# The first layer of 128-row expert blocks as seven products of row halves, on one Trainium2 core

## The chip, the cores and the metric

The kernel runs on one core of a Trainium2 chip. A core has engines that run side by side, each through its own queue in order: TensorE (PE, with its weight loads as PEld), VectorE (DVE), ScalarE (ACT), GpSimd (POOL) and SyncE (SP), and DMA queues. They wait for each other by semaphores. The metric is the device time of one execution in microseconds; three runs of the kernel before gave 626.19, 626.38 and 627.47, median 626.38.

## What is computed

Causal attention over a window of 64 positions, for 8 batches of 576 positions and 8 heads of 64, gives x with 8 x 576 = 4608 rows of 512. Then each row goes to one of eight experts:

```
logits = x @ w_gate                       # 512 -> 8
local  = sigmoid(x @ w_local)
e      = argmax(logits) if s == 0 or local < 0.5 else e of the row before
p      = softmax(logits)
h      = maximum(x @ w1[e], 0)            # 512 -> 1024
out    = p[e] * (h @ w2[e])               # 1024 -> 512
```

All in float32. Which rows belong to which expert is known only while the kernel runs.

## The kernel before

The attention part writes x to DRAM and works out each row's expert. Then the rows of each expert are cut into blocks, and each block fetches its rows by indirect DMAs (gathers, issued by POOL) and the two weight matrices of its expert by DMAs from SP's queue (2 MB each). There are four kinds of block:

- large, 256 rows (two slots of 128), numbers below `NB`;
- of 128 rows (one slot), numbers from `NB` to below `KINDS[1]`; four of them stand in the order of this program;
- of 64 rows (halves), from `KINDS[1]` to below `KINDS[2]`;
- of 32 rows (quarters), from `KINDS[2]`.

The order is made by `run`: large blocks one after the other, and behind every second one a smaller block. A block of 128 rows always stands between two large ones. `rows` sets the kind of a block in a dictionary `st`: `rows` (rows of a slot), `big`, `fast1` and `fast2` (whether the first and the second layer go by seven products).

Each block goes through four steps. `turn` (VectorE) transposes the gathered rows into `st["xt"]`, 128 partitions x 4 x rows: x turned, so that the contraction lies on the partitions. `prepare` (VectorE, where `fast1` is set) makes the sums and differences that the seven products need. `hidden` is the first layer and writes `h`, 128 x 8 x rows. `result` is the second layer, scales it by p[e] and scatters the rows to the output.

Seven products: a matrix product cut into quarters needs eight products of quarters; by Winograd's form of Strassen's scheme seven will do, with sums of quarters of the one matrix (`ws`, from `left`), differences of quarters of the other (`xs`, from `right`), and additions of the products. `big_hidden` does this for x @ w1: it cuts w1 by its contraction (two halves of 256) and its columns (two halves of 512), and x by contraction and by rows. Three PSUM banks, `px`, `py`, `pz`, hold the products; ScalarE keeps copies of three of them in SBUF (`keep`), VectorE adds a copy to a later product, ScalarE applies the relu, and so the four quarters of h, `hq[i][j]` (i: half of the 1024 columns, j: half of the rows), are made one after the other, from the fourth, fifth, sixth and seventh product. `big_result` does the same for h @ w2; its `put` is a VectorE instruction that scales and adds a piece of the output, three in a block, and between its products it calls hooks, in which VectorE's work for the next block is issued. The fifth of these hooks, behind the second `put`, makes the sums `s3` and `s4` of the next block if `turn` left them for later (`rest`).

A block of 128 rows has neither: its first layer is the plain loop in `hidden`, 8 x 4 matmuls of 128x128 weights against 128 columns, in two PSUM tiles. The first is emptied by ScalarE while the second is filled, the second by VectorE (`tensor_relu`, L1525). Its second layer is the plain loop at the end of `result`, 8 matmuls with 512 columns, of which the first four read the first half of `h`'s columns and the last four the second half. A block of 64 rows runs the same loop in `hidden` with `st["rows"]` = 64: the weights of a 128-column tile are cut in two halves of 64 columns, which write partitions 0 to 63 and 64 to 127 of PSUM (side by side).

In this part of the kernel all engines run in the order in which the code is written (`manual_schedule`). The names `ws1`, `xs` and `keep0` to `keep2` are single buffers. A gather is released by the matmul at which `pace` is called: in `hidden` behind every second column tile, in `big_hidden` behind every product.

## Time and profile before

One execution was profiled: it took 627.78 us, of which the span from the first to the last instruction is 626.0 us.

| | |
|---|---|
| median of three runs | 626.38 us |
| the profiled execution | 627.78 us |
| its span | 626.0 us |
| TensorE's mean granted clock | 0.999 |
| bytes moved by DMA | 165.80 MB, mean 265 GB/s |

The attention part fills about the first quarter of the span, the experts the rest. In the profile's lists "x64" counts records; a float32 matmul leaves two of them, with a weight load each. A row of an order of time gives the start, the time from there to the end of the last record merged into the row, engine, line, operation, and in brackets the idle time before it and what ended it. Matmuls overlap at their ends, so lengths are best read from start to start. A row of the groups by line gives, behind the bar, the busy time in us, the mean of one record in ns, and the idle time before.

### The profile page before, as it was taken

The numbers are of one execution on the slowest core, as the hardware profiler recorded it, in microseconds if no ns is written. First come the engines' busy times: TensorE is split into PE (matmuls) and PEld (weight loads), VectorE is DVE, ScalarE is ACT, GpSimd is POOL, SyncE is SP. The second block draws the span as 40 slices with busy tenths as digits, with TensorE's granted clock in tenths as the row PEclk, the third lists the DMA queues.
The fourth block names the chain that finished last, engine by engine and source line by source line (L and its number), as shares of the span: only waits on it lengthen the run. The fifth ranks groups of instructions, "written<-read, shape, count | busy, mean of one in ns | idle before, by whom it ended". The sixth has DMA issues, their size and how long they took to land. (4 is left out here: it accounts for less than half of the span.)

```text
span 626.0 us, 15072 instructions
## 1 busy us (share of the span) xinstructions
PE 600.5 (96%) x6253; PEld 528.9 (84%) x6253; DVE 403.2 (64%) x757; ACT 200.5 (32%) x368; POOL 271.4 (43%) x261
## 2 busy tenths in 40 slices
PE   7888988999999999999999999999999999999995
PEld 6677766788889999979899799978997998999994
DVE  6567579888996767347381885183926763886730
ACT  3766755722382232203130123112221322123120
POOL 4432111622102567437146775175275866452001
PEclk9999999999999999999999999999999999999999
DMA  8999998787945557476967866687768656955601
GB/s 328 401 415 407 365 378 284 273 304 250 385 153 186 190 210 281 170 272 246 394 245 259 321 198 217 230 314 300 299 239 316 256 189 223 403 193 208 233 18 40
DMA packets 31880, 165.80 MB, mean 265 GB/s; under 512 B 10531, under 2 KB 12217, under 8 KB 22586
## 3 DMA queue, kind: packets, MB, share of 16 engines
q1 hardware_dynamic: 20394, 135.54, 58.6%
q0 software_dynamic: 11408, 29.20, 13.0%
q8 instruction: 51, 0.84, 0.5%
q14 instruction: 27, 0.22, 0.1%
HBM read 145.52 MB, written 19.59 MB: 264 GB/s over the span
## 5 line engine op out<-in xcount | busy, mean ns | idle before, releaser
L1184 POOL DMA_INDIRECT xg<-xs,g x118 | 134.2, 1138 | 46.0 <-issue 25.3
L1494 POOL DMA_INDIRECT out_dram<-y,idx x36 | 41.1, 1142 | 161.3 <-DVE y L1425 68.5
L1414 PE MATMUL hp<-ws,hs 128*128 128x256 f32 x384 | 88.9, 380 | 0.0
L1414 PEld LDWEIGHTS hp<-ws,hs 128*128 128x128 f32 x384 | 72.5, 190 | 10.9 <-issue 1.2
L1363 PE MATMUL hp<-xs,ws 128*128 128x128 f32 x672 | 79.7, 275 | 0.0
L1363 PEld LDWEIGHTS hp<-xs,ws 128*128 128x128 f32 x672 | 77.3, 192 | 0.1
L1425 DVE SCALAR_TENSOR_TENSOR y<-hp,pws,kept 128x256 f32<-128x256 f32 x48 | 23.2, 482 | 68.2 <-issue 41.2
L1514 PE MATMUL hp<-xt,w 128*64 128x64 f32 (+2 forms) x640 | 66.2, 276 | 0.0
L1514 PEld LDWEIGHTS hp<-xt,w 128*128 128x128 f32 (+1 forms) x640 | 60.8, 170 | 4.1 <-issue 0.7
L1414 PE MATMUL hp<-w,h 128*128 128x256 f32 x256 | 60.5, 379 | 0.0
L1375 DVE TENSOR_TENSOR h<-hp,keep 128x512 f32<-128x512 f32 x42 | 28.6, 689 | 43.9 <-PE hp L1363 43.1
L1363 PEld LDWEIGHTS hp<-xt,w 128*128 128x128 f32 x448 | 53.2, 192 | 2.7 <-issue 2.3
L1363 PE MATMUL hp<-xt,w 128*128 128x128 f32 x448 | 54.7, 275 | 0.0
L394 PEld LDWEIGHTS sp<-w 64*64 64x64 f32 x1296 | 39.1, 135 | 16.2 <-issue 11.2
L1414 PEld LDWEIGHTS hp<-w,h 128*128 128x128 f32 x256 | 47.3, 190 | 5.7
L425 ACT ACTIVATE p<-sp 128x512 f32<-128x512 f32 x72 | 39.1, 596 | 37.1 <-PE sp L394 34.8
L440 PE MATMUL xo<-vb,p 128*64 128x74 f32 (+1 forms) x576 | 44.0, 228 | 6.9 <-DVE x L450 3.0
L394 PE MATMUL sp<-w 64*64 64x128 f32 (+1 forms) x1296 | 45.1, 267 | 5.7 <-issue 4.5
L430 DVE TENSOR_TENSOR p<-p,mask 128x1024 f32<-128x1024 f32 x29 | 35.8, 1235 | 22.4 <-ACT p L425 22.3
L1184 POOL DMA_INDIRECT pws<-xw,gx x40 | 44.3, 1107 | 13.2 <-issue 8.5
L440 PEld LDWEIGHTS xo<-vb,p 128*64 128x64 f32 x576 | 38.3, 136 | 12.6 <-issue 5.2
L1376 ACT ACTIVATE h<-h 128x512 f32<-128x512 f32 x42 | 26.3, 630 | 60.1 <-DVE h L1375 60.1
(287 smaller groups left out, 977.5 us busy)
## 6 DMA issues: line engine op xcount, KB each, us to landing
w<-in_w_dram SPq DMA_DIRECT2D x22, 2048.0 KB, 9.4
w<-in_w1t_dram SPq DMA_DIRECT2D x20, 2048.0 KB, 8.7
w<-in_kq_dram SPq DMA_DIRECT2D x17, 1024.0 KB, 11.2
w<-in_w_dram SPq DMA_DIRECT2D x24, 512.0 KB, 8.5
xs<-x POOLq DMA_DIRECT2D x9, 1024.0 KB, 5.9
va<-in_v_dram SPq DMA_DIRECT2D x5, 1184.0 KB, 7.5
vtt<-in_vt_dram SPq DMA_DIRECT2D x5, 1024.0 KB, 6.2
va<-in_v_dram SPq DMA_DIRECT2D x3, 1040.0 KB, 15.5
```

The source lines that it names most:

```text
L394: nc.tensor.matmul(sp[j][c * WIN:(c + 1) * WIN, a:b], lhsT=kt[h, hp, block * WIN:(block + 1) * WIN], rhs=qt[h, hp, a:b], start=not biased, ...
L425: nc.scalar.activation(p[:, j], sp[j], Act.Exp, scale=DH ** -0.5)
L430: masked.append(nc.vector.tensor_tensor(p, p, m.to_broadcast([P, 2, SC]), op=Alu.mult))
L440: nc.tensor.matmul(xo[par * WIN:(par + 1) * WIN, j, s * VW:s * VW + n], lhsT=p[:, j, b * WIN:(b + 1) * WIN], rhs=w[:, s, 2 * hp + j, :n], ...
L1184: return self.nc.gpsimd.indirect_dma_start(out=out, out_offset=None, in_=table[:rows, :], in_offset=bass.IndirectOffsetOnAxis(ap=idx, axis=0))
L1363: mm = nc.tensor.matmul(out[:, m, :], lhsT=a[:, kk, m * P:(m + 1) * P], rhs=b[:, kk, :], start=start and m + kk == 0, stop=stop and (m, kk ...
L1375: nc.vector.tensor_tensor(o, x, y, op=add)
L1376: nc.scalar.activation(o, x if y is None else o, Act.Relu)
L1414: mm = nc.tensor.matmul(out, lhsT=a[:, m, :], rhs=b[:, m, :], start=start and m == 0, stop=stop and m == FK // 2 - 1, skip_group_check=True)
L1425: nc.vector.scalar_tensor_tensor(o, x, pw[i], y2, Alu.mult, Alu.add)
L1494: return self.nc.gpsimd.indirect_dma_start(out=self.out[:, :], out_offset=bass.IndirectOffsetOnAxis(ap=st["idx"][:, s:s + 1], axis=0), in_ ...
L1514: mm = nc.tensor.matmul(hp[a, i, :], lhsT=st["w1"][:, kk, m * P:(m + 1) * P][:, a], rhs=st["xt"][:, kk, :n], start=(kk == 0), stop=(kk == ...
```

## The change

Blocks of 128 rows (`fast1` now depends on `n < KINDS[1]`, so all blocks with 128 rows in a slot) do their first layer by `big_hidden`, with row halves of 64 instead of 128 (`st["wide"]`). Each product has 4 column tiles x 2 contraction steps, and each matmul is cut in two with 64 weight columns, which write the two halves of the partitions. The second layer stays plain, so `prepare2` and `halves`, which serve it, are left out for these blocks. `sums` keeps the size of its tile and hands out a narrower part.

```diff
@@ rows
-        st.update(x=[], slots=slots, idx=idx, rows=P, big=len(slots) == 2, fast1=len(slots) == 2 and n not in PLAIN1,
+        st.update(x=[], slots=slots, idx=idx, rows=P, big=len(slots) == 2, fast1=n < KINDS[1] and n not in PLAIN1,
                   fast2=len(slots) == 2 and n not in PLAIN2)
+        st["wide"] = P if st["big"] else HF
@@ prepare
-        st["xq"] = quarters(st["xt"], DK, BIG)
+        c = 2 * st["wide"]
+        st["xq"] = quarters(st["xt"][:, :, :c], DK, c)
         st["xt"] = self.right("xs", st["xq"])
@@ sums
-        t = self.one.tile([P, 4, a[0][0].shape[1], a[0][0].shape[2]], F32, name=name)
-        return [t[:, i] for i in range(4)]
+        n, c = a[0][0].shape[1:]
+        t = self.one.tile([P, 4, n, max(c, P)], F32, name=name)
+        return [t[:, i, :, :c] for i in range(4)]
@@ big_hidden
-        self.prepare2(st)
+        if st["fast2"]:
+            self.prepare2(st)
+        n, c = FK // 2, st["wide"]
         st["h"] = h = self.wk.tile([P, FK, BIG], F32, name="h", bufs=1)
-        st["hq"] = hq = quarters(h, FK, BIG)
-        n = FK // 2
-
-        pz, py, px = (self.ps_h.tile([P, n, P], F32, name="hp") for _ in range(3))
+        st["hq"] = hq = quarters(h[:, :, :2 * c], FK, 2 * c)
+
+        pz, py, px = (self.ps_h.tile([P, n, P], F32, name="hp")[:, :, :c] for _ in range(3))
 
         def product(out, a, b, start=True, stop=True):
             for m in range(n):
                 for kk in range(DK // 2):
-                    mm = nc.tensor.matmul(out[:, m, :], lhsT=a[:, kk, m * P:(m + 1) * P], rhs=b[:, kk, :],
-                                     start=start and m + kk == 0,
-                                     stop=stop and (m, kk) == (n - 1, DK // 2 - 1), skip_group_check=True)
+                    for f in range(0, P, c):
+                        mm = nc.tensor.matmul(out[f:f + c, m, :], lhsT=a[:, kk, m * P + f:m * P + f + c],
+                                              rhs=b[:, kk, :], start=start and m + kk == 0,
+                                              stop=stop and (m, kk) == (n - 1, DK // 2 - 1), skip_group_check=True)
             self.pace(mm)
 
         def keep(i, x):
-            o = self.one.tile([P, n, P], F32, name=f"keep{i}")
+            o = self.one.tile([P, n, P], F32, name=f"keep{i}")[:, :, :c]
...
         relu(hq[1][0], px)
         step()
-        self.halves(st)
+        if st["fast2"]:
+            self.halves(st)
```

The lines shift by up to six: L1363 of before is L1368 of the change, L1566 is L1572, L1425 is L1431, L1514 is L1520.

TensorE's queue in the first block of 128 rows before: the plain first layer (L1514, into `hp`) and the second layer (L1566, into `yp`), each row with the semaphores for which its first matmul waits.

```order
L1514 MATMUL hp<-xt,w 128x128 [waits DMAHW1_49]
L1514 MATMUL hp<-xt,w 128x128 x15
L1514 MATMUL hp<-xt,w 128x128 [waits DVE_49]
L1514 MATMUL hp<-xt,w 128x128 x15
L1566 MATMUL yp<-w,h 128x512 [waits DMAHW2_49,Activation_49]
L1566 MATMUL yp<-w,h 128x512 x3
L1566 MATMUL yp<-w,h 128x512 [waits DVE_49]
L1566 MATMUL yp<-w,h 128x512 x3
```

The same place of the change, from the third product on:

```order
L1368 MATMUL hp<-xs,ws_3507 64x64 [waits Activation_49]
L1368 MATMUL hp<-xs,ws_3507 64x64 x15
L1368 MATMUL hp<-xt,w 64x64 x16
L1368 MATMUL hp<-xs,ws_3507 64x64 [waits Activation_49]
L1368 MATMUL hp<-xs,ws_3507 64x64 x15
L1368 MATMUL hp<-xt,ws_3507 64x64 x16
L1368 MATMUL hp<-xs,w 64x64 [waits DVE_49]
L1368 MATMUL hp<-xs,w 64x64 x15
L1572 MATMUL yp<-w,h 128x512 [waits DMAHW2_49,Activation_49]
L1572 MATMUL yp<-w,h 128x512 x3
L1572 MATMUL yp<-w,h 128x512 [waits Activation_49]
L1572 MATMUL yp<-w,h 128x512 x3
```

Thirty-two matmuls of 128x128 become seven products of sixteen with 64x64; products wait for ScalarE's copies and VectorE's additions, and the second layer's first matmul waits for a later relu of ScalarE than before, since both row halves must be there.

VectorE's queue ahead of the same block and in it, before: the transpose of its rows, the three `put` of the large block ahead (L1425), the relu (L1525).

```order
L1283 STREAM_TRANSPOSE xt<-xg 128x4x4x32 [waits DMASW2_49,DMASW3_49,DMASW1_49,DMASW0_49]
L1425 SCALAR_TENSOR_TENSOR y<-hp,pws,kept_3512 128x256 [waits DMASW1_49,DMASW6_49,PE_49,Activation_49]
L1425 SCALAR_TENSOR_TENSOR y<-hp,pws,kept_3518 128x256 [waits DMASW4_49,DMASW7_49,PE_49,Activation_49]
L1425 SCALAR_TENSOR_TENSOR y<-hp,pws,kept_3524 128x256 [waits PE_49,Activation_49]
L1525 TENSOR_SCALAR h<-hp 128x4x128 [waits DVE_49,PE_49]
```

In the change, behind the same transpose:

```order
L1328 TENSOR_TENSOR xs<-xt 128x2x64
L1328 TENSOR_TENSOR xs<-xt,xs 128x2x64 [waits DVE_49]
L1314 TENSOR_TENSOR ws_3507<-w 128x1024 [waits DMAHW1_49]
L1314 TENSOR_TENSOR ws_3507<-ws_3507,w 128x1024 [waits DVE_49]
L1431 SCALAR_TENSOR_TENSOR y<-hp,pws,kept_3520 128x256 [waits DMASW1_49,DMASW6_49,PE_49,Activation_49]
L1431 SCALAR_TENSOR_TENSOR y<-hp,pws,kept_3526 128x256 [waits DMASW4_49,DMASW7_49,PE_49,Activation_49]
L1314 TENSOR_TENSOR ws_3507<-w 128x1024
L1314 TENSOR_TENSOR ws_3507<-w,ws_3507 128x1024 [waits DVE_49]
L1431 SCALAR_TENSOR_TENSOR y<-hp,pws,kept_3532 128x256 [waits PE_49,Activation_49]
L1380 TENSOR_TENSOR h<-hp,keep_3591 128x4x64 [waits PE_49,Activation_49]
L1380 TENSOR_TENSOR h<-hp,keep_3612 128x4x64 [waits PE_49,Activation_49]
L1380 TENSOR_TENSOR h<-hp,keep_3631 128x4x64 [waits PE_49]
```

Four differences of rows and two sums of weights (the last two of the differences and the sums are the rows shown first) now stand ahead of the first `put`, two more sums between the second and the third `put`, and three additions take the place of the relu.

## The prediction

> **What bounds the kernel.** I read the page first, then the table by stage for the four stretches in which a block of 128 rows is worked, then TensorE's order of time there, and last the other engines' order of time at the same places.

> ```profile
> span 626.0 us, 15072 instructions
> PE 600.5 (96%) x6253; PEld 528.9 (84%) x6253; DVE 403.2 (64%) x757; ACT 200.5 (32%) x368; POOL 271.4 (43%) x261
> PE   7888988999999999999999999999999999999995
> ```

> TensorE is busy for 96% of the span, and in all but the last of the slices behind the first quarter its digit is 9: the expert part is bound by it. The four blocks of 128 rows lie in this part; here are the first and the last of the four stretches, each from the block's first matmul to that of the next block (columns: length, then busy time of PE, PEld, DVE, ACT, POOL, the granted clock, the DMA share).

> ```profile
> 267.96:281.97 14.01, 14.01 (x81) 10.19 (x80) 6.56 (x10) 1.07 (x2) 5.67 (x6) 1.00 0.80 298
> 467.30:481.31 14.01, 14.01 (x81) 10.19 (x80) 6.57 (x10) 1.07 (x2) 7.60 (x8) 1.00 0.84 320
> ```

> PE is busy for all of the 14.01 us, at full clock, so time that goes from its queue here goes from the end, and a wait put into it comes on top. The second block, as PE sees it:

> ```profile
> 334.31 1.89 PE L1414 MATMUL hp<-ws,h 128*128 128x256 f32 x8
> 336.03 7.31 PE L1514 MATMUL hp<-xt,w 128*128 128x128 f32 x64
> 343.18 7.03 PE L1566 MATMUL yp<-w,h 128*128 128x512 f32 x16
> 350.05 1.95 PE L1363 MATMUL hp<-xt,w 128*128 128x128 f32 x16
> ```

> Lengths go from start to start, since the ends overlap. The first layer takes 343.18 - 336.03 = 7.15 us: 32 matmuls in the code, 64 records, because each float32 matmul leaves two. The second layer takes 6.87 us and isn't changed. So the change acts on 4 x 7.15 = 28.6 us of 626.

> **What TensorE is given instead.** Seven products of 4 x 2 x 2 matmuls are 112 matmuls, 224 records, each with 64 columns of weights and 64 rows. Blocks of 64 rows have run matmuls of just this shape all along, also two side by side:

> ```profile
> 528.77 1.89 PE L1414 MATMUL hp<-ws,h 128*128 128x256 f32 x8
> 530.59 3.95 PE L1514 MATMUL hp<-xt,w 128*64 128x64 f32 x128
> 534.37 3.63 PE L1544 MATMUL yp<-w,h 128*64 128x256 f32 x32
> 537.93 2.05 PE L1363 MATMUL hp<-xt,w 128*128 128x128 f32 x16
> ```

> 128 records take 534.37 - 530.59 = 3.78 us, 29.5 ns each; a record of the old form took 7.15 / 64 = 111.7 ns for four times the work, which is 27.9 ns a quarter. Seven eighths of the arithmetic at 1.06 times the price: 224 x 29.5 = 6.61 us, 0.945 us for a product. The gross gain is 0.54 us a block, 2.2 us in all. Everything below is about how much of that is eaten.

> **Going in and out of the narrow form.** The eight records before 336.03 take 1.72 us. Before the narrow block the same eight start at 528.77 and the narrow ones at 530.59, 1.82 us: 0.10 us lost on the way in; I charge 0.09. On the way out, 32 narrow records of 256 elements run at half of 1.72 / 8 = 0.215 us each, 3.45 us, while 537.93 - 534.37 = 3.56: 0.11 us. [...]

> **The wait that is added.** Before, the second layer started with the part of `h` that ScalarE had written while the other half of the first layer still ran. Now its first matmul needs both row halves, and the second of these, `hq[0][1]`, comes out of the sixth of seven products: VectorE adds, ScalarE applies the relu, and only the seventh product covers that. The rows from which I price this chain, of other places:

> ```profile
> 534.59 0.42 DVE L1525 TENSOR_SCALAR h<-hp 128x256 f32<-128x256 f32 x1 [1.44 <-PE hp L1514]
> 292.89 0.69 DVE L1375 TENSOR_TENSOR h<-hp,keep 128x512 f32<-128x512 f32 x1 [1.02 <-PE hp L1363]
> 293.62 0.63 ACT L1376 ACTIVATE h<-h 128x512 f32<-128x512 f32 x1 [1.08 <-DVE h L1375]
> L1376 ACT ACTIVATE h<-h 128x512 f32<-128x512 f32 x39 | 24.4, 630 | 54.9 <-DVE h L1375 54.9
> L1376 ACT ACTIVATE h<-hp 128x512 f32<-128x512 f32 x13 | 7.8, 597 | 6.5 <-PE hp L1363 6.5
> L1466 ACT ACTIVATE qh<-yp 128x256 f32<-128x256 f32 x2 | 0.8, 383 | 2.8 <-PE yp L1462 2.8
> ```

> VectorE starts 534.59 - 534.37 = 0.22 us after the next matmuls do, and a 128x256 piece takes 0.42. ScalarE starts 293.62 - 292.89 - 0.69 = 0.04 later. Its relu of 128x256 took 0.383 us from PSUM; from SBUF it is slower by 630 - 597 = 33 ns, so 0.416. Counted from the start of the seventh product, h is there at 0.22 + 0.42 + 0.04 + 0.42 = 1.10 us, and the product is through at 0.945. What such a wait costs PE is shown once, where VectorE came late:

> ```profile
> 320.72 1.88 DVE L1375 TENSOR_TENSOR h<-hp,keep 128x512 f32<-128x512 f32 x3
> 319.86 1.95 PE L1363 MATMUL hp<-xt,ws 128*128 128x128 f32 x16
> 322.05 2.05 PE L1363 MATMUL hp<-xs,w 128*128 128x128 f32 x16 [0.24 <-DVE h L1375]
> 323.94 1.89 PE L1414 MATMUL hp<-w,h 128*128 128x256 f32 x8
> ```

> Three adds in 1.88 us start 0.595 apart, so the second ended at 322.00, and PE started 0.05 later; then its 16 records took 1.89 instead of 1.79 us, 0.10 more to fill again, since the weight load too had waited. So the wait costs 1.10 + 0.05 - 0.945 + 0.10 = 0.30 us. The matmul that waits has the rest of the second layer behind it and then the next block, all in one queue. From below the cost is 0 (the chain fits after all); from above, if the pieces of 128x256 took as long as those of 128x512, it is 0.22 + 0.69 + 0.04 + 0.63 + 0.05 - 0.945 + 0.10 = 0.79 us. I take 0.30, since the 128x256 rows are the nearer ones. The way out (0 to 0.11 us) falls into this wait, so I don't charge it again.

> **Waits inside the products.** Banks are used again two products later, with 0.945 us between where a product of a large block has 16 x 111.7 ns = 1.79. A copy by ScalarE takes 0.22 + 0.38 + 0.05 = 0.65 us to its release, an add by VectorE 0.22 + 0.42 + 0.05 = 0.69. Both fit: nothing, as long as VectorE is free at that moment.

> **What VectorE gets to do, and where.** Its rows around the second block:

> ```profile
> 325.83 0.71 DVE L1283 STREAM_TRANSPOSE xt<-xg 128x512 f32<-128x512 f32 x1
> 331.11 0.48 DVE L1425 SCALAR_TENSOR_TENSOR y<-hp,pws,kept 128x256 f32<-128x256 f32 x1 [4.57 <-issue]
> 332.83 0.48 DVE L1425 SCALAR_TENSOR_TENSOR y<-hp,pws,kept 128x256 f32<-128x256 f32 x1 [1.24 <-PE hp L1414]
> 334.57 0.48 DVE L1425 SCALAR_TENSOR_TENSOR y<-hp,pws,kept 128x256 f32<-128x256 f32 x1 [1.26 <-PE hp L1414]
> 343.38 0.69 DVE L1525 TENSOR_SCALAR h<-hp 128x512 f32<-128x512 f32 x1 [8.32 <-PE hp L1514]
> 343.98 1.29 DVE L1283 STREAM_TRANSPOSE xt<-xg 128x512 f32<-128x512 f32 x2
> 345.31 0.42 DVE L1326 TENSOR_TENSOR xs<-xt 128x256 f32<-128x256 f32 x1
> 346.78 1.22 DVE L1312 TENSOR_TENSOR ws<-w 128x1024 f32<-128x1024 f32 x1
> 349.18 1.22 DVE L1312 TENSOR_TENSOR ws<-w 128x1024 f32<-128x1024 f32 x1
> ```

> Ahead of the first `put` come four differences of rows and two sums of weights. In a large block these take 346.78 - 345.31 = 1.47 us (256 wide, here 128) and 349.18 - 346.78 = 2.40: at most 3.87 us, into an idle stretch of 4.57. The other two sums stand between the second and the third `put`, as they do where a large block follows a large one:

> ```profile
> 240.17 0.48 DVE L1425 SCALAR_TENSOR_TENSOR y<-hp,pws,kept 128x256 f32<-128x256 f32 x1 [0.72 <-issue]
> 242.84 0.48 DVE L1425 SCALAR_TENSOR_TENSOR y<-hp,pws,kept 128x256 f32<-128x256 f32 x1
> ```

> There the third starts 2.67 us after the second; here that is 335.50 instead of 334.57, ended at 335.98. The second product writes that `put`'s bank, at 336.03 + 0.09 + 0.945 = 337.07: a cover of 1.09 us. If it were gone, each microsecond of lateness would be one of PE's. In the block itself VectorE idled for 8.32 us, in which the three adds of 0.42 stand. It then turns to the next block's transposes at 336.12 + 6 x 0.945 + 0.64 = 342.43 instead of 343.98, so the next block gets its sums earlier. ScalarE has 1.07 us of work in 14 and takes three copies and three relus more. The sums of weights read `w1` some 9 us before PE did:

> ```profile
> 305.78 0.33 SPq L1261 DMA_DIRECT2D w<-in_w1t_dram  x1
> w<-in_w1t_dram SPq DMA_DIRECT2D x20, 2048.0 KB, 8.7
> ```

> The load for the second block was issued at 305.78 and with 8.7 us is there 13 us before VectorE asks at about 328. POOL's gathers are released at 11 points of the block instead of 8, earlier rather than later; PE waits for none of them.

> **The sum.** Per block 0.09 + 6.61 + 0.30 = 7.00 us against 7.15: 0.15 us less, four times 0.6 us. The profiled execution took 627.78 us, 1.8 around its span, and would take 627.2; it lies 1.4 above the median of the runs, so in medians 626.38 - 0.6 = 625.8 us. A measurement of this kernel can tell about 0.2% from no change, 1.25 us; the forecast is **no difference that can be told**, with 625.1 to 627.0 as its own range (way out charged on top: 626.2; chain 0.2 us longer or shorter: 0.8 either way).

> **Rivals.** First, the wait doesn't show: h is ready when the seventh product ends. Then a block takes 0.09 + 6.61 = 6.70, 0.45 less, 1.8 us in all: 624.6, faster. For it speaks that the excess is only 0.15 us before the restart is charged; against it the restart row, and that each link is a measured row. Second, on the other side: the short products don't cover the emptying of their banks. If pieces of 128x256 with gaps between their rows cost what the 128x512 ones do, the wait before the second layer is 0.79, and the seventh product waits for the add before it too: 0.22 + 0.69 + 0.05 - 0.945 + 0.10 = 0.12. A block takes 0.09 + 6.61 + 0.12 + 0.79 = 7.61, 0.46 more, 1.8 us in all: 628.2. It becomes slower by 0.2% once the overheads of a block pass 0.85 us (7.15 - 6.61 + 0.31), against 0.39 in my sum. Against it: the 0.42 row is of a piece with such gaps. Third, that the change doesn't reach what runs: excluded, as the order shows it in all four blocks, and rows of L1566 show that these run.

> **How the numbers follow.** The forecast 0.68, the first rival 0.18, the second 0.10, and 0.04 for something larger on either side. Faster by over 0.2% (below 625.1): 0.19; slower (above 627.6): 0.13; between: 0.68. The range reaches down to the first rival's time and half way to the second's: 624.4 to 627.3.

> **What would show it.** In the profile after: four groups of 224 narrow records with 6.6 us from the first to the last; an idle entry of 0.2 us or so before the first matmul of the second layer, put down to ScalarE's relu; VectorE's third `put` before such a block about 1 us later, and nobody waiting for it. Wrong would be: a record pitch other than 29.5 ns, idle entries inside the seven products, or the sums of weights still running when the second product starts.

## The result

The change makes the kernel slower: 633.76 us in the median of four runs, 626.29 for the kernel before beside it; the ratio is 1.0118, interval 1.0099 to 1.0136. The forecast was 625.8 and no difference, with a range up to 627.3.

The page of the changed kernel, with the row of the DMA queue that carries "instruction", which the prediction didn't read; in the kernel before this row was `q8 instruction: 51, 0.84, 0.5%`.

```profile
span 631.4 us, 16439 instructions
...
PE 599.6 (95%) x6893; PEld 526.4 (83%) x6893; DVE 428.0 (68%) x797; ACT 209.3 (33%) x392; POOL 269.3 (43%) x261
...
q8 instruction: 56, 0.92, 0.6%
```

TensorE is busy for less time than before (600.5) in a longer span, so it waits. The four stretches of the 128-row blocks, in the table by stage (length, then the busy time of PE, PEld, DVE, ACT, POOL):

```profile
266.77:282.56 15.79, 13.91 (x241) 9.89 (x241) 9.28 (x14) 3.23 (x8) 7.62 (x7) 1.00 0.74 271
336.67:352.86 16.19, 13.99 (x241) 9.89 (x241) 8.57 (x13) 3.22 (x8) 9.73 (x10) 1.00 0.77 288
402.14:417.29 15.15, 13.72 (x241) 9.76 (x241) 9.92 (x15) 3.23 (x8) 7.22 (x7) 1.00 0.81 310
471.40:486.88 15.48, 13.98 (x241) 9.89 (x241) 8.57 (x13) 3.22 (x8) 9.42 (x9) 1.00 0.79 297
```

They were 14.0 us each. The four make 62.61 against 56.06 us, and with 0.10 us each on the way in 6.9 us more: about the whole difference of the medians, 7.5. (The spans differ by 5.4 only, since this profiled execution came to its first such block 1.2 us sooner.) Where it goes, in TensorE's order of time for the second block:

```profile
334.85 1.89 PE L1420 MATMUL hp<-ws,h 128*128 128x256 f32 x8
336.67 1.15 PE L1368 MATMUL hp<-xt,w 128*64 128x64 f32 x32
337.65 2.04 PE L1368 MATMUL hp<-xs,ws 128*64 128x64 f32 x64
339.52 1.10 PE L1368 MATMUL hp<-xt,w 128*64 128x64 f32 x32
340.45 1.10 PE L1368 MATMUL hp<-xs,ws 128*64 128x64 f32 x32
341.39 0.40 PE L1368 MATMUL hp<-xt,ws 128*64 128x64 f32 x7
343.95 0.97 PE L1368 MATMUL hp<-xt,ws 128*64 128x64 f32 x25 [2.17 <-issue]
344.71 1.15 PE L1368 MATMUL hp<-xs,w 128*64 128x64 f32 x32
345.89 7.13 PE L1572 MATMUL yp<-w,h 128*128 128x512 f32 x16
```

In the middle of the sixth product, behind 7 of its 32 records, TensorE stands still for 2.2 us, and "issue" says that nothing in the profile released it. A product has no wait inside. The list of waits of PE has these rows:

```profile
PE hp L1368 <- issue: 5.5, 3, 2.2
...
PE yp L1572 <- ACT h L1381: 1.4, 1, 1.4
```

Three blocks stop inside a product; the third stops at the first matmul of the second layer, and there the list names ScalarE. The last relu in ScalarE's order of time in that block:

```profile
408.47 0.42 ACT L1381 ACTIVATE h<-h 128x256 f32<-128x256 f32 x1 [0.45 <-DVE h L1380]
```

The first matmuls behind it in PE's:

```profile
410.32 7.13 PE L1572 MATMUL yp<-w,h 128*128 128x512 f32 x16 [1.43 <-ACT h L1381]
```

The relu had ended at 408.89, 1.43 us before PE went on: the engine named had long been done, and it was the same thing there.

```profile
q1 hardware_dynamic: 139, 2.08, 89.8%
q0 software_dynamic: 43, 0.17, 6.2%
q14 instruction: 1, 0.01, 0.6%
...
q0 software_dynamic: 60, 0.14, 37.3%
q8 instruction: 1, 0.02, 5.5%
q1 hardware_dynamic: 4, 0.02, 4.0%
```

Up to 272.7 the 2 MB of a weight load pass (queue 1); only when that is nearly through comes the fetch (in the four blocks, 1.85 to 2.08 of the load's 2.10 MB had been begun by then). Its start, found in this way in all four blocks, and where PE stopped and went on:

| block | load's first packet | fetch starts | took | PE stops | PE goes on |
|---|---|---|---|---|---|
| 1 | 266.11 | 272.76 | 0.88 | 272.9 | 274.98 |
| 2 | 336.02 | 341.47 | 1.22 | 341.6 | 343.95 |
| 3 | 401.48 | 407.93 | 0.94 | 408.7 | 410.32 |
| 4 | 470.74 | 476.00 | 1.07 | 476.8 | 478.44 |

From the start of the fetch to PE's going on it is 2.2 to 2.5 us each time. And counting all of PE's instructions in the trace from the beginning (matmul records, weight loads and the waits between them), with n fetches begun before this one, PE has begun 256 n + 449 of them when it stops, in all four blocks: it looks as if it had used up what was fetched. That gave the theory (A): the narrow products use 256 instructions in 3.8 us (128 records at 29.5 ns), a fetch waits behind the weight load that starts with the block, and TensorE runs out of program.

### The profile page after: what moved, and what is told of

Its sections match the earlier page's. It is cut to its first block, busy times and chain, and to the rows that moved or that the text cites. A ratio compares the mean times of both kernels' runs of the same rounds, so it can differ in the third digit from the quotient of the medians.

```text
span 631.4 us, 16439 instructions
## 1 busy us (share of the span) xinstructions
PE 599.6 (95%) x6893; PEld 526.4 (83%) x6893; DVE 428.0 (68%) x797; ACT 209.3 (33%) x392; POOL 269.3 (43%) x261
## 5 line engine op out<-in xcount | busy, mean ns | idle before, releaser
L1184 POOL DMA_INDIRECT xg<-xs,g x118 | 132.8, 1125 | 43.7 <-issue 26.2
L1368 PE MATMUL hp<-xs,ws 128*128 128x128 f32 (+1 forms) x1056 | 92.3, 256 | 0.0
L1368 PEld LDWEIGHTS hp<-xs,ws 128*128 128x128 f32 (+1 forms) x1056 | 89.2, 173 | 0.1
L1380 DVE TENSOR_TENSOR h<-hp,keep 128x512 f32<-128x512 f32 (+1 forms) x54 | 33.7, 631 | 76.2 <-PE hp L1368 74.1
L1368 PEld LDWEIGHTS hp<-xt,w 128*128 128x128 f32 (+1 forms) x704 | 61.3, 172 | 4.0 <-issue 3.6
L1368 PE MATMUL hp<-xt,w 128*128 128x128 f32 (+1 forms) x704 | 63.7, 257 | 0.0
L1431 DVE SCALAR_TENSOR_TENSOR y<-hp,pws,kept 128x256 f32<-128x256 f32 x48 | 23.1, 482 | 49.0 <-issue 24.5
L1381 ACT ACTIVATE h<-h 128x512 f32<-128x512 f32 (+1 forms) x54 | 31.3, 583 | 71.9 <-DVE h L1380 71.9
L1375 ACT COPY keep<-hp 128x512 f32<-128x512 f32 (+1 forms) x54 | 29.1, 539 | 59.1 <-PE hp L1368 59.1
L440 PE MATMUL xo<-va,p 128*64 128x74 f32 (+1 forms) x576 | 44.1, 228 | 2.4 <-issue 2.4
## 6 DMA issues: line engine op xcount, KB each, us to landing
w<-in_w_dram SPq DMA_DIRECT2D x22, 2048.0 KB, 9.3
w<-in_w1t_dram SPq DMA_DIRECT2D x20, 2048.0 KB, 8.7
```

What stands on the lines that cost most here:

```text
L440: nc.tensor.matmul(xo[par * WIN:(par + 1) * WIN, j, s * VW:s * VW + n], lhsT=p[:, j, b * WIN:(b + 1) * WIN], rhs=w[:, s, 2 * hp + j, :n], ...
L1184: return self.nc.gpsimd.indirect_dma_start(out=out, out_offset=None, in_=table[:rows, :], in_offset=bass.IndirectOffsetOnAxis(ap=idx, axis=0))
L1368: mm = nc.tensor.matmul(out[f:f + c, m, :], lhsT=a[:, kk, m * P + f:m * P + f + c], rhs=b[:, kk, :], start=start and m + kk == 0, stop=sto ...
L1375: nc.scalar.copy(o, x)
L1380: nc.vector.tensor_tensor(o, x, y, op=add)
L1381: nc.scalar.activation(o, x if y is None else o, Act.Relu)
```

## The experiments

The rivals were a fetch that is late by itself (A'), and waits of the seven products for the other engines, or VectorE's sums (B). Each run is compared with the kernel before, run beside it: 626.62 us for the first four experiments (`e1` to `e4`), 627.66 for the rest.

**The loads held.** Of the two loads for the next block the second, and what stands behind it in SP's queue, waits for the last narrow product.

```diff
@@ run, in the loop over blocks
-                if i + 2 < len(order):
-                    self.weights(jobs[i + 2], order[i + 2])
+                if i + 2 < len(order) and not one_slot(n):
+                    self.weights(jobs[i + 2], order[i + 2], names=("w1", ) if one_slot(order[i + 1]) else ("w1", "w2"))
...
+            if one_slot(n):
+                self.weights(jobs[i + 1], order[i + 1], names=("w2", ), hold=jobs[i]["mm"])
+                self.weights(jobs[i + 2], order[i + 2])
...
```

> The change, with the two weight loads that follow (the second matrix of the next block and what stands behind it in SP's queue) held until the last narrow product. Theory A (TensorE runs out of instructions in the narrow products, because the fetch of the next 16 KB of its program waits behind the 2 MB weight load that starts with the block): the idle of 1.4 to 2.4 us a block goes, 625.5 to 627.0 us. Theory A' (it runs out, but the fetch is late by itself, load or no load): still 632 to 635. Theory B (the products wait for copies, additions or sums of the other engines): still 632 to 635, with idle entries put down to them.

627.24 us against 626.62, ratio 1.0016 (0.9997 to 1.0035): 0.2 us above the range expected by A, and far below that of A' and B. The first block in PE's order of time:

```profile
266.32 1.89 PE L1424 MATMUL hp<-ws,h 128*128 128x256 f32 x8
268.14 1.15 PE L1371 MATMUL hp<-xt,w 128*64 128x64 f32 x32
...
273.79 1.10 PE L1371 MATMUL hp<-xs,w 128*64 128x64 f32 x32
274.93 7.13 PE L1576 MATMUL yp<-w,h 128*128 128x512 f32 x16
281.90 1.95 PE L1371 MATMUL hp<-xt,w 128*128 128x128 f32 x16
```

No stop; 13.76 us from 268.14 to 281.90, and 13.76 or 13.77 in all four blocks. The fetch came at 270.94, 2.8 us into the block instead of 6.0. A stands; A' and B, by which the stop would stay, fall.

**Half the instructions.** In `product` the cut of the weights is taken out: 128 columns against 64 rows, 112 records.

```diff
-                    for f in range(0, P, c):
-                        mm = nc.tensor.matmul(out[f:f + c, m, :], lhsT=a[:, kk, m * P + f:m * P + f + c],
...
+                    mm = nc.tensor.matmul(out[:, m, :], lhsT=a[:, kk, m * P:(m + 1) * P],
...
```

> The change with 128 columns of weights for 64 rows: 112 records a block instead of 224, half the instructions. Theory A: no idle of over a microsecond; the time is then set by the pitch of such a record, which no run shows yet: at 59 ns (two narrow ones) 626, at 112 ns (as with 128 rows) 5.5 us a block more, 648. Theory B: idle entries inside the products remain, put down to ScalarE or VectorE.

648.22 us, ratio 1.0347 (1.0321 to 1.0374), with no stop over 0.2 us in its four blocks. The seventh product of the first block:

```profile
276.98 1.95 PE L1367 MATMUL hp<-xs,w 128*128 128x64 f32 x16
278.77 7.08 PE L1571 MATMUL yp<-w,h 128*128 128x512 f32 x16
```

16 records take 1.79 us, 112 ns each, as with 128 rows: with 128 columns of weights, halving the rows didn't shorten a record (112 ns against 111.7), while two records of 64 columns and 64 rows take 59 ns together. The narrow form is what makes row halves of 64 worth anything, and it uses nearly four times the instructions per microsecond (112 against 29.5 ns a record). That no stop is left is what A expects, but records so slow would hide a late fetch in any case (an estimate: 256 instructions, 128 records, last 128 x 112 ns = 14.3 us there), so this run says little on A.

**The sums alone.** VectorE makes the sums and differences, and the first layer stays plain.

```diff
-        c = 2 * st["wide"]
+        c, st["whole"] = 2 * st["wide"], st["xt"]
...
-        if st["fast1"]:
+        if st["fast1"] and st["big"]:
             return self.big_hidden(st, step)
+        if st["fast1"]:
+            st["xt"] = st["whole"]
```

> VectorE's eight sums and differences for each 128-row block are made as in the change but not used; the first layer is the plain loop of before. Theory A: 626 to 627, since VectorE's added work is hidden. Theory B in the form that the sums cost: 630 to 634.

627.16 us, ratio 1.0017 (1.0000 to 1.0034), 0.2 us above what A expected; the four blocks take 14.01 or 14.02 us, as before. VectorE's work is hidden.

**Narrow pieces without the scheme.** The plain first layer of the kernel before, cut in 64 columns by 64 rows: nothing to add, to copy or to wait for.

```diff
-                for kk in range(DK):
-                    for f in range(0, P, st["rows"]):
+                for r in range(0, n, cut):
+                    for kk in range(DK):
+                        for f in range(0, P, wide):
...
```

> The kernel before, with the plain first layer of 128-row blocks cut into 64 columns of weights by 64 rows: 128 matmuls, 256 records a block, no sums, no copies, no additions. By the pitch of 29.5 ns alone 7.55 us a block, 0.4 more than before, 628. Theory A: on top 1.4 to 2.4 us of idle a block, put down to nothing that the profile shows: 633 to 638. Theory B: 628.

637.12 us, ratio 1.0161 (1.0139 to 1.0182). PE in the third block:

```profile
408.76 4.57 PE L1517 MATMUL hp<-xt,w 128*64 128x64 f32 x96 [2.35 <-issue]
```

The blocks take 16.26, 14.59, 18.70 and 16.62 us, and the second has no stop: there a fetch had begun 1.6 us ahead of the block, and the next wasn't needed in it. The three stops lie at 256 n + 449 again. So the scheme of seven products has no part in it; the stop follows the fetch. In the third block the stop is not all: its last 96 records take 4.49 us to the second layer, where 29.2 ns each would be 2.8. The table by stage shows why:

```profile
409.80:413.25 3.45, 3.45 (x67) 3.33 (x63) 0.00 (x0) 0.00 (x0) 1.98 (x2) 0.51 0.22 81
```

The 0.51 is the granted clock: for 3.4 us from 409.8 on it was 0.5, and a record took 53 ns; in no other block of any profiled run did the narrow records slow down so. What lowered the clock there isn't shown.

**The same, with the loads held.** The edit of the first experiment on top of this one.

> The plain first layer in 64x64 pieces (as e4_plain_64x64), with the loads held as in e1_hold_load, until the last piece of the block. Theory A: the idle of 1.4 to 2.4 us goes; 0.5 us a block is left over the kernel before, 628 to 629. If the idle in that run came from the form of the products and not from the fetch behind the load: 635 to 638.

630.12 us against 627.66, ratio 1.0031 (1.0005 to 1.0057); all four blocks take 14.58 or 14.59 us, without a stop. The time lies 1.1 us above the range expected, but the kernel before was slower too in these runs: 2.5 us lie between the two, and the blocks, with 0.10 us each on the way in, explain 2.7. A once more.

**Half the load held.** The first megabyte goes at once, the second waits.

```diff
-            m = a * b // (PARTS if n < 0 else 1)
+            m = a * b // (PARTS if n < 0 else 2 if halved and name == "w2" else 1)
...
+                if halved and name == "w2" and c:
+                    st["piece"] = piece
+                    continue
...
```

> The change; of the 2 MB load that starts with each 128-row block the first half (1 MB) goes as in the change and only the second half, with the loads behind it, is held until the last narrow product. Theory A (the fetch of instructions starts only when the load ahead of it has nearly passed): the fetch that came 5 to 7 us after the load began comes 2 to 4 us after it, early enough; no idle of over 1 us, 625.5 to 628. Theory A2 (any running load, whatever its length, puts the fetch off by some 5 us): the idle stays, 632 to 635.

626.74 us against 627.66, ratio 0.9997 (0.9976 to 1.0018). The fetches start 2.8 to 3.4 us into the blocks instead of 4.6 to 6.0. Counted from the load's first packet it is 3.4 to 4.1 us instead of 5.3 to 6.6, there about when the half load's last packet starts (3.6 to 4.0). So the length of the load ahead counts, and A2 falls. In the second block 143 instructions were left at that moment by the same count, the fewest of the four, and there a product took 0.4 us longer, with a short halt at 256 n + 449:

```profile
338.24 1.52 PE L1381 MATMUL hp<-xt,ws 128*64 128x64 f32 x32
339.54 1.15 PE L1381 MATMUL hp<-xs,w 128*64 128x64 f32 x32
```

143 instructions last 143 x 14.7 ns = 2.1 us, the fetch needs 2.2 to 2.5: a halt of 0.1 to 0.4 us by the count, which fits this one.

**The load let go with the fourth product.** One index differs from the first experiment.

```diff
-            st["mm"] = mm
+            st.setdefault("mm", []).append(mm)
...
-                self.weights(jobs[i + 1], order[i + 1], names=("w2", ), hold=jobs[i]["mm"])
+                self.weights(jobs[i + 1], order[i + 1], names=("w2", ), hold=jobs[i]["mm"][3])
...
```

> As e1_hold_load, but the load is let go with the fourth of the seven products, 3.8 us into the block. Theory A: the fetch for this block is asked for 1.8 us into it and goes ahead of the load; no idle, 625.5 to 628. If what matters is that a load runs while the narrow products do, asked for before or after: an idle stays, above 630.

625.34 us against 627.66, ratio 0.9976 (0.9953 to 0.9998), 0.2 us below the range expected. The first and the last of its blocks:

```profile
264.13:277.90 13.77, 13.73 (x242) 9.77 (x242) 8.58 (x14) 3.23 (x8) 10.11 (x9) 1.00 0.72 270
...
462.96:476.73 13.77, 13.73 (x242) 9.76 (x241) 8.58 (x14) 3.23 (x8) 10.72 (x11) 1.00 0.73 270
```

The fetches start 1.3 to 3.3 us into the blocks, ahead of the load, which in the first block was issued 4.0 us into it (268.12 - 264.13). Behind the fetch the load ran beside narrow products and did no harm: all four blocks took 13.76 or 13.77 us, as with the load held to the end.

**The kernel before, loads held.** The control.

> The kernel before, with the loads held as in e1_hold_load until the last matmul of the plain first layer. All theories: within 0.2% of the kernel before, 625.5 to 627.5; what it costs to hold the loads is then nothing.

626.87 us against 627.66, ratio 0.9986 (0.9968 to 1.0005), blocks of 14.01 us: to hold the loads costs nothing and brings nothing that can be told.

## Why the prediction was wrong

The step that failed is the gross term, "224 x 29.5 = 6.61 us". The pitch was right: in the products without a stop 0.93 us each, 29.2 ns a record. What was wrong was to carry it from 128 records to 224. The 64-row blocks' 128 records are 256 instructions, the length of one fetch, and in their rows no stop lies; 448 instructions in one go need the next fetch inside. The prediction's "Waits inside the products" put such waits at nothing, and looked only at banks that have to be emptied; that TensorE's own program could be late was in none of its terms. The term has to be 6.61 plus the stop, 1.4 to 2.4 us: the blocks took 15.79, 16.19, 15.15 and 15.48 us, without a stop 13.76. That is 7.6 us in all, and the forecast of -0.6 becomes +7.0; measured, +7.5. One of the signs that the prediction gave for being wrong came, idle entries inside the seven products, and the time fell into the 0.04 that it had left for something larger on either side.

Two rows could have told it. The page showed queue 8 as a queue of its own, with packets of 16 KB. And the list of PE's waits in the kernel before had entries "issue" of up to 1.4 us in the attention part, where matmuls of 64x64 and 128x64 stand; I looked at the expert part only, where there were none:

```profile
PE sp L394 <- issue: 4.5, 6, 1.4
PE xo L440 <- issue: 3.3, 5, 1.0
```

They are of the same kind. Counted in the same way, each of these eleven stops lies at 256 n + 449 (or one more), and PE goes on 2.3 to 2.6 us after a fetch began. So by this count the kernel before already stood still for 7.8 us for want of its program, about as much as the change lost by it (7.6). Whether holding back a load would help there wasn't tried.

Point by point, the rest held:

- The way in cost 336.67 - 334.85 - 1.72 = 0.10 us, charged 0.09.
- The wait before the second layer: from the start of the seventh product to the second layer 345.89 - 344.71 = 1.18 us, and the second layer 6.97 instead of 6.87; together 0.34 us over 0.945 and 6.87, charged 0.30. Without the stop (`e1_hold_load`, first block) the chain is the forecast one: the add starts 0.21 us after the seventh product, the relu ends at 1.09, PE goes on at 1.14, where the prediction has 1.10 + 0.05. The idle entry that it expected isn't listed, since the product's last record is shown ending just before. The 0.10 of the second layer stands in `e6_plain_held` too (6.97), where no late relu is waited for, so it belongs to the way out as much as to the wait; the sum is the same.
- The block without the stop, 13.76 + 0.10 = 13.86 us against 14.01, is 0.15 less: the sum of the prediction, to the hundredth, in two kernels (`e1_hold_load`, `e7_hold_4th`). The parts fit too: the seven products take 0.98 + 6 x 0.93 = 6.56 us for 6.61, the wait and the longer second layer 0.31 for 0.30.
- VectorE's sums cost nothing (`e3_sums_only`: 14.01 or 14.02 us a block, as before). In the third block of the change its third `put` came 2.67 us after the second, as forecast, and nobody waited for it:

```profile
398.85 0.48 DVE L1431 SCALAR_TENSOR_TENSOR y<-hp,pws,kept 128x256 f32<-128x256 f32 x1 [1.24 <-PE hp L1420]
399.25 1.22 DVE L1314 TENSOR_TENSOR ws<-w 128x1024 f32<-128x1024 f32 x1
...
401.52 0.48 DVE L1431 SCALAR_TENSOR_TENSOR y<-hp,pws,kept 128x256 f32<-128x256 f32 x1
```

- The rival on the slower side, banks that don't empty in time, didn't come: ScalarE's copies of 128x256 took 0.37 us and the additions 0.42, as priced. The slower side came from a mechanism that no rival named.

What stays open: where the fetch waits. It started later with a longer load ahead of it (4.6 to 6.0 us into the block with 2 MB, 2.8 to 3.4 with 1 MB), but the runs don't show which queue or engine holds it back. And the blocks explain a gain of 0.6 us, 0.1%, for `e1_hold_load` and `e7_hold_4th` alike; the first measured 0.16% slower than the kernel before, the second 0.24% faster with an interval that ends near 1. That the change with the loads held is faster than the kernel before isn't shown.

## What to carry over

The pitch of the narrow matmuls wasn't their whole price here: they also used up program, and at 29.5 ns a record the 256 instructions of a fetch were used in 3.8 us. Before such a stretch is made longer than the one its pitch was read from, count its instructions against 256 to a fetch (448 in a block here, with stops of 1.4 to 2.4 us), and look what DMA starts at that moment. If a load stands in front of the fetch, let it go some microseconds later: `e7_hold_4th` let it go 4.0 us into its first block and had no stop in any of the four. In a list of waits, entries "issue" before small matmuls (4.5 and 3.3 us in the kernel before), or a wait put down to an engine that had long been done (1.43 us in the third block), are places to look for it.

## What the runs showed of the hardware

- 640 records and 640 weight loads more came with 5 packets of 16 KB more on queue 8 (51 in the kernel before, 56 in the change). PE stopped 449 instructions past 256 times the number of earlier fetches, in all four blocks of the change and, within one instruction, at the eleven "issue" entries of the kernel before. It went on 2.2 to 2.6 us after the next fetch began.
- With a 2 MB weight load ahead of it that fetch began 4.6 to 6.0 us into the block (the change), with half of it 2.8 to 3.4 (`e5_half_load`), with none 1.9 to 3.1 (2.8 in the first block of `e1_hold_load`).
- A float32 matmul with 128 columns of weights took 112 ns a record with 64 rows (`e2_wide_weights`) as with 128 (111.7 in the kernel before); with 64 columns and 64 rows, two side by side, it took 29.2 to 29.5 ns a record.
- In one block of `e4_plain_64x64` the granted clock was 0.5 for 3.4 us behind a stop of 2.35 us, and narrow records took 53 ns.
